# Decay attention, then a GELU MLP: the last 64 queries of batches 3 to 7 as one AV run of two heads side by side

## The chip, the core and the metric

The kernel runs on one core of one Trainium2 chip. The metric is the device time of one execution in microseconds (us). A profile records one execution: when each engine was busy, what ended its idle time, and what the DMA engines moved. The engines are TensorE (in the profile PE, its weight loads PEld), VectorE (DVE), ScalarE (ACT), GpSimd (POOL) and SyncE (SP), which issues most of the DMAs. Each engine works through its own instructions in their order; engines wait for each other through semaphores. Matmuls write to PSUM, which has eight banks of 512 fp32 columns; everything else lies in SBUF.

## The reference

Eight batches, eight heads, 576 tokens, 64 columns a head. Scores get a decay from the cumulative sum of log f and a causal mask; the attention's output, all heads side by side, is the input x of an MLP with exact GELU (512 to 2048 to 512).

```python
log_f = np.log(np.clip(f, 0.0001, 1.0))
cum = np.cumsum(log_f, axis=-1)
decay = cum[:, :, :, None] - cum[:, :, None, :]
scores = np.where(causal, -1e9, scale * q @ k.T + decay)
attn = softmax(scores)                      # over the keys
x = (attn @ v).transpose(0, 2, 1, 3).reshape(B * S, H * D)
out = gelu(x @ w_in) @ w_out
```

The decay of a query cancels in the softmax. The kernel multiplies v by a weight per key instead (`wT`) and carries the weight itself as a 65th column of v, which gives the softmax's sum.

## The kernel before

**Blocks.** 576 tokens are 4.5 blocks of 128. The key blocks and the query blocks begin at `K0 = [0, 128, 256, 384, 448]`: the fifth block of queries, 448 to 575, repeats 64 queries of the fourth. gemm1 of a batch takes the first 512 tokens of x (`TC`). The last 64 tokens (`TL`) of all eight batches are gathered in one tile `tails`, 8 x 64 = 512 columns for each of four groups of 128 rows of x, and go through the MLP at the very end, as a ninth "batch" (`gemm1(B, ...)`, `gemm2(B)`).

**Order.** The schedule is written out by hand: instructions are issued in the order of the program, and each engine keeps its part of it. Batches 0 and 1 have code of their own (`first_attention`, `second_attention`). From batch 2 on, `attention(b)` does, for each of four pairs of heads `i`, four score tiles (`scores`, L319 on TensorE, exp on ScalarE at L329, causal mask on GpSimd at L331). Between them come pieces of gemm2 of the batch before (`take(fill, n)`, L509). From batch 3 on, AV of all four pairs follows: `av(0)`, `av_both(b, 1)`, `av_both(b, 2)`, `av(3)`, then the last eleven steps of gemm2, then gemm1 of this batch (`gemm1_open`, then `gemm1`, all at L405).

**AV.** `attend` (L350) does, for a head and query block m, one matmul for each key block n up to m: the stationary operand is 128 columns of the tile of exponentials `e`, the moving one the 65 columns of weighted v. So the blocks take 1 + 2 + 3 + 4 + 5 = 15 matmuls a head. `normalize` (L363, L364) or the end of `av_both` (L838, L839) divides on VectorE into a tile `x` in SBUF; the pool of these tiles has four. `x_dma` (L389) then has SP issue a transposing DMA of five blocks of 128x128 into `xT`, pair by pair. `x_tail` (L395) is a copy on GpSimd of the last 64 columns of `xT` into `tails`, behind all transposes.

**Who holds PSUM.** `s_psum` has two slots of two banks: score tiles, the outputs of `av_both`, and in `gemm1_open` four accumulators. `o_psum` has two banks (`av`, and `spare()` in gemm1), `m_psum` two (gemm2, gemm1). `gemm1_open` takes two slots of `s_psum`, two of `o_psum` and one of `m_psum` at once for seven column groups, and does the first two of the four row groups of x for six of them, so that the transposes of the later pairs have time to land. A copy of gemm2's last group (`put_off`, L906) is held back behind the divisions of AV, and the last addition and store of gemm2 (L533, L537) come after it.

**Batch 0** already treats its last 64 queries apart (`attend_tail`, L689): two heads of a pair write to the lower and the upper 64 partitions of one bank, with stationary operands of 64 columns. `tail_0` transposes that on TensorE.

Of the kernel before, what the change touches and what calls it, by code (L numbers as in the profile page):

```python
# [9 lines left out]
FP32 = mybir.dt.float32  # L10
BF16 = mybir.dt.bfloat16
Act = mybir.ActivationFunctionType
Alu = mybir.AluOpType
PSUM = bass.MemoryType.PSUM

P = 128
S = 576
D = 64
H = 8
HP = 4  # L20
NBLK = 5
K0 = [0, 128, 256, 384, 448]
TC = 512
# [18 lines left out]
def where(n, m):  # L42

    q = K0[m]
    for t, parts in enumerate(STILES):
        c = 0
        for nn, q0, w in parts:
            if nn == n and q0 <= q and q + P <= q0 + w:
                return t, c + q - q0
            c += w  # L50
    raise KeyError((n, m))
# [3 lines left out]
def kernel(  # L55
# [10 lines left out]
    nc = tc.nc  # L66
    B = q.shape[0]
# [3 lines left out]
    n_dm = d_model // P  # L71
    n_ff = d_ff // P
    n_sub = TC // P
    XC = NBLK * P
    TL = S - TC
# [5 lines left out]
    consts = ctx.enter_context(tc.tile_pool(name="consts", bufs=1))  # L81
# [5 lines left out]
    x_pool = ctx.enter_context(tc.tile_pool(name="x", bufs=4))  # L87
# [3 lines left out]
    s_psum = ctx.enter_context(tc.tile_pool(name="s_psum", bufs=2, space=PSUM))  # L91
# [119 lines left out]
                ps[:, 0:w], warm[:, 0:P], warm[:, 0:w], start=True, stop=True  # L211
            )

    tails = consts.tile([P, n_dm, TC], BF16)


    def transposes_first(b, i, pool, tag, both=(0, 1), parts=1):
# [58 lines left out]
    vw_of = {}  # L276
# [20 lines left out]
    e_of = {}  # L297
# [43 lines left out]
    o_of, x_of, xT_of = {}, {}, {}  # L341

    def attend(b, i, h, ms, pool=o_psum, tag="o"):
        if (b, i, h) not in o_of:
            o_of[b, i, h] = pool.tile([P, NBLK, D + 1], FP32, tag=tag, name="o")
        o = o_of[b, i, h]
        for m in ms:
            for n in range(m + 1):
                t, c = where(n, m)
                nc.tensor.matmul(  # L350
                    o[:, m, :],
                    e_of[b, i, t][:, h, c : c + P],
                    vw_of[b][:, 2 * i + h, n, :],
                    start=(n == 0),
                    stop=(n == m),
                )

    def normalize(b, i, h):
        if (b, i) not in x_of:
            x_of[b, i] = x_pool.tile([P, NBLK, 2, D], BF16, tag="x", name="x")  # L360
        o = o_of[b, i, h]
        r = x_pool.tile([P, NBLK], FP32, tag="r", name="r")
        nc.vector.reciprocal(r, o[:, :, D])  # L363
        nc.vector.tensor_tensor(  # L364
            x_of[b, i][:, :, h, :],
            o[:, :, 0:D],
            r.unsqueeze(2).to_broadcast([P, NBLK, D]),
            Alu.mult,
        )

    def xT(b):
        if b not in xT_of:
            xT_of[b] = xT_pool.tile([P, n_dm, XC], BF16, tag="xT", name="xT")
        return xT_of[b]
# [11 lines left out]
        copy(xT(b)[:, i, :], ps)  # L386

    def x_dma(b, i):
        nc.sync.dma_start_transpose(  # L389
            xT(b)[:, i, :].rearrange("d (m p) -> d m p", p=P),  # L390
            x_of[b, i].rearrange("p m h d -> p (m h d)"),
        )

    def x_tail(b):
        nc.gpsimd.tensor_copy(tails[:, :, b * TL : (b + 1) * TL], xT(b)[:, :, XC - TL :])  # L395


    g_of = {}

    def gemm1(c, ffb, kts=range(4), ps=None, act=True):  # L400
        src = xT(c) if c < B else tails
        if ps is None:
            ps = m_psum.tile([P, TC], FP32, tag="m", name="ps1")
        for kt in kts:
            nc.tensor.matmul(  # L405
                ps,
                w_in_sb[:, kt, ffb * P : (ffb + 1) * P],
                src[:, kt, 0:TC],
                start=(kt == 0),
                stop=(kt == n_dm - 1),  # L410
            )
        if n_dm - 1 in kts and act:
            gelu(c, ffb, ps)
        return ps

    def spare():
        return o_psum.tile([P, TC], FP32, tag="o", name="ps1")

    def gelu(c, ffb, ps):
        if c not in g_of:  # L420
            g_of[c] = [
                g_pool.tile([P, TC], BF16, tag=f"g{n}", name=f"g{n}")
                for n in range(n_ff)
            ]
        nc.scalar.activation(g_of[c][ffb], ps, Act.Gelu)  # L425
# [159 lines left out]
    def gemm2_third():  # L585
        yield from gemm2_second(0)
        yield from gemm2_rows(0, PLAN_0)
        yield from gemm2_rows(1, PLAN_1)

    def take(gen, n):  # L590
        for _ in range(n):
            if next(gen, "end") == "end":
                return
# [68 lines left out]
            x_of[0, i] = x_pool.tile([P, NBLK, 2, D], BF16, tag="x", name="x")  # L662
        divide(x_of[0, i][:, 0 : TC // P, h, :], o, TC // P)

    def divide(x, o, n):
        r = x_pool.tile([P, NBLK], FP32, tag="r", name="r")
        nc.vector.reciprocal(r[:, 0:n], o[:, 0:n, D])
        nc.vector.tensor_tensor(
            x,
            o[:, 0:n, 0:D],  # L670
            r[:, 0:n].unsqueeze(2).to_broadcast([P, n, D]),
            Alu.mult,
        )

    def to_xT_0(i, copy):
        ps = m_psum.tile([P, TC], BF16, tag="m", name="ps_x")
        for m in range(TC // P):
            nc.tensor.transpose(
                ps[:, m * P : (m + 1) * P], x_of[0, i][:, m, :, :], ident_bf
            )  # L680
        copy(xT(0)[:, i, 0:TC], ps)
# [18 lines left out]
    def tail_0():  # L700
        ps = o_psum.tile([P, HP, TL], BF16, tag="o", name="ps_x")
        for i in range(HP):
            for h in range(2):
                d = slice(h * D, (h + 1) * D)
                nc.tensor.transpose(
                    ps[d, i, :], x_of[0, "tail"][d, i, :], ident_bf[d, d]
                )
        nc.vector.tensor_copy(tails[:, :, 0:TL], ps)

    def first_attention():  # L710

# [116 lines left out]
    def av_both(b, i):  # L828


        st = s_psum.tile([P, 2, 512], FP32, tag="s", name="o2")
        both = st[:, :, 0 : NBLK * (D + 1)].rearrange("p h (m d) -> p h m d", m=NBLK)
        for h in range(2):
            o_of[b, i, h] = both[:, h]
            attend(b, i, h, (0, 1, 2, 3, 4))
        x_of[b, i] = x_pool.tile([P, NBLK, 2, D], BF16, tag="x", name="x")
        r = x_pool.tile([P, 2, NBLK], FP32, tag="r2", name="r2")
        nc.vector.reciprocal(r, both[:, :, :, D])  # L838
        nc.vector.tensor_tensor(  # L839
            x_of[b, i].rearrange("p m h d -> p h m d"),  # L840
            both[:, :, :, 0:D],
            r.unsqueeze(3).to_broadcast([P, 2, NBLK, D]),
            Alu.mult,
        )
        x_dma(b, i)
# [21 lines left out]
    def attention(b):  # L867


        fill = gemm2_third() if b == 2 else gemm2_rows(b - 1, PLAN)  # L870
        counts = FILL_2 if b == 2 else FILL

        def av(i, n=0):
            for h in range(2):
                attend(b, i, h, (0, 1, 2, 3, 4))
                normalize(b, i, h)
                if h == 0:
                    take(fill, n)
            x_dma(b, i)

        for i in range(HP):
            for t in range(4):
                scores(b, i, t)
                take(fill, counts[i][t])
                if t == 1 and b == 2 and i > 0:
                    av(i - 1)
                    if i == 1:
                        load_v(3)
                if b == 2 and (i, t) == (0, 3):
                    weigh_v(b, 2)  # L890
                    weigh_v(b, 3)
                if b > 2 and i == 0 and t == 1:
                    load_v(b + 1)
                if b > 2 and t == 0 and i < 2:
                    transpose_dma(b + 1, 4 * i, 4 * i + 4)
                if b == 2 and t == 1 and i == 1:
                    transpose_dma(3, 0, 4)
        if b == 2:
            take(fill, 4)
            av(HP - 1)  # L900
        else:
            av(0)
            av_both(b, 1)
            av_both(b, 2)
            av(3)
            put_off.pop()()  # L906
        if b == 2:
            take(fill, 4)
            transpose_dma(3, 4, 8)
        take(fill, 999)  # L910

        if b == 2:
            pss = [gemm1(b, ffb, (0, 1)) for ffb in range(2)]
            pss += [spare(), spare()]
            for ffb in range(2):
                gemm1(b, ffb, (2,), pss[ffb])
            for ffb in (2, 3):
                gemm1(b, ffb, (0, 1, 2), pss[ffb])
            for ffb in range(4):
                gemm1(b, ffb, (3,), pss[ffb])  # L920
            more = s_psum.tile([P, 2, 512], FP32, tag="s", name="ps1")
            gemm1(b, 4, ps=more[:, 0, :])
        else:
            gemm1_open(b)
        if b + 1 < B:
            untangle(b + 1, 0)
            weigh_v(b + 1, 0)
        x_tail(b)

    def second_attention():  # L930

# [133 lines left out]
```

## Time and profile before

| what | before |
|---|---|
| time, median of 3 runs (lowest to highest) | 332.75 us (332.35 to 337.22) |
| the profiled execution: its time, its span | 332.24 us, 330.5 us |
| granted TensorE clock | 0.999 |
| AV, L350, on TensorE | 840 matmuls, 29.0 us busy |
| batch 0's tail, L689, on TensorE | 40 matmuls, 0.8 us busy |
| gemm1, L405, from x and from the tails | 512 matmuls, 114.0 us; 64 matmuls, 14.3 us |
| GpSimd's copies into the tails, L395 | 7, 3.4 us busy, 29.1 us idle before them |
| transposes of x, L389, on SP | 24, 2.7 us from issue to landing (median) |

The busy time of a group is the time in which at least one of its instructions was running. Matmuls overlap in the pipeline: one of 512 columns lasts 379 ns in the records, while the next starts 216 ns after it. So costs on TensorE are read from start to start. The chain that ended last follows the work back from the end of the execution, at each step to what released it; an engine that is not on it can be late by some amount without any effect.

### The profile page before, as it was taken

What the parts mean: (1) busy time and instruction counts of PE and PEld (TensorE: products, weight loads), DVE (VectorE), ACT (ScalarE), POOL (GpSimd) and SP (SyncE); (2) the same over time, 40 slices, a digit from 0 to 9 for tenths busy, and PEclk for the clock granted to TensorE, in tenths of its full rate; (3) what the DMA queues carried; (4) which work ended last, traced back from release to release, by engine and by line L of the source; (5) the groups of instructions that cost most, each with busy time, mean ns of one, the idle gap of its engine ahead of it and who ended that gap; (6) DMA issues with size and microseconds to landing.
All of it is one profiled execution on the core that took longest, in us unless ns stands there. A gap on an engine that the chain in (4) does not pass through costs nothing.

```text
span 330.5 us, 8129 instructions
## 1 busy us (share of the span) xinstructions
PE 322.2 (97%) x3327; PEld 173.0 (52%) x3327; DVE 184.6 (56%) x412; ACT 203.0 (61%) x296; POOL 134.5 (41%) x260
## 2 busy tenths in 40 slices
PE   8999999999999999999999999999999999999995
PEld 4664555445554467445744565456645574444443
DVE  5952766754649637993599359954995370010011
ACT  4986886965526894289718980899078926305600
POOL 8997873067346153525344443635152500000000
PEclk9999999999999999999999999999999999999999
DMA  7999999959999699399968996699600141020022
GB/s 125 194 195 220 208 193 147 207 122 220 199 194 178 101 227 140 84 157 179 213 94 117 189 219 117 94 172 236 122 15 2 66 96 48 0 97 32 0 54 76
DMA packets 94949, 44.19 MB, mean 134 GB/s; under 512 B 74176, under 2 KB 89792, under 8 KB 94912
## 3 DMA queue, kind: packets, MB, share of 16 engines
q1 hardware_dynamic: 77760, 27.16, 42.5%
q0 software_dynamic: 16752, 15.99, 30.3%
q8 instruction: 26, 0.43, 0.6%
q10 hardware_dynamic: 400, 0.52, 0.4%
q14 instruction: 11, 0.09, 0.1%
HBM read 36.85 MB, written 9.44 MB: 140 GB/s over the span
## 4 chain that ended last, share of the span: by engine, by line
PE 94%; ACT 2%; DMA 1%; DVE 1%; issue 1%; SPq 0%; DVEq 0%
PE ps L405 38%; PE ps L509 27%; PE ps L449 8%; PE o L350 8%; PE s L319 6%; DMA xT<-x 1%; PE s L623 1%; PE ps_w L210 1%; ACT e L628 1%; PE ps_f L226 1%; PE ps L573 1%; PE ps L549 1%; PE o L654 1%; ACT e L329 0%; PE ps_x L383 0%
## 5 line engine op out<-in xcount | busy, mean ns | idle before, releaser
L425 ACT ACTIVATE g<-ps 128x512 bf16<-128x512 f32 x138 | 75.8, 618 | 87.3 <-PE ps L405 86.1
L405 PE MATMUL ps<-xT,w_in_sb 128*128 128x512 bf16 x512 | 114.0, 379 | 0.8 <-DMA xT<-x 0.6
L509 PE MATMUL ps<-w_out_sb,g 64*128 64x512 bf16 (+1 forms) x751 | 106.3, 376 | 0.0
L329 ACT ACTIVATE e<-s 128x896 bf16<-128x896 f32 x112 | 87.8, 836 | 14.4 <-PE s L319 9.9
L405 PEld LDWEIGHTS <-w_in_sb 128*128 128x128 bf16 x576 | 55.3, 98 | 67.2 <-issue 2.1
L331 POOL TENSOR_SCALAR_AFFINE_SELECT e<-e 128x256 bf16<-128x256 bf16 (+1 forms) x135 | 49.1, 383 | 76.6 <-ACT e L329 76.3
L509 PEld LDWEIGHTS <-g 64*128 64x128 bf16 (+1 forms) x751 | 42.6, 94 | 32.2 <-issue 1.3
L288 POOL TENSOR_TENSOR vw<-v_sb,wT 128x640 bf16<-128x640 f32 (+1 forms) x30 | 38.3, 1276 | 29.4 <-DMA v_sb<-in_v_dram 14.9
L269 DVE COPY qT<-tq 64x288 bf16<-64x288 bf16 x96 | 44.1, 459 | 3.5 <-DMA tq<-q 2.0
L523 DVE COPY ot<-ps 128x512 f32<-128x512 f32 x20 | 13.8, 692 | 52.8 <-PE ps L509 52.8
L269 DVE COPY kT<-tk 64x288 bf16<-64x288 bf16 x96 | 38.3, 399 | 2.7 <-DMA tk<-k 1.1
L319 PE MATMUL s<-qT,kT 64*128 64x256 bf16 (+1 forms) x336 | 37.8, 275 | 0.8 <-DVE kT L241 0.6
L458 DVE COPY ot<-ps 128x512 f32<-128x512 f32 (+2 forms) x9 | 5.7, 632 | 49.5 <-PE ps L449 49.5
L350 PEld LDWEIGHTS <-e 128*128 128x128 bf16 x840 | 27.9, 98 | 4.3 <-issue 2.4
L350 PE MATMUL o<-vw,e 128*128 128x65 bf16 x840 | 29.0, 194 | 0.0
L319 PEld LDWEIGHTS <-kT 64*128 64x128 bf16 x336 | 18.1, 94 | 19.8 <-issue 4.0
L449 PE MATMUL ps<-w_out_sb,g 128*128 128x512 bf16 (+2 forms) x144 | 28.0, 355 | 0.0
L449 PEld LDWEIGHTS <-g 128*128 128x128 bf16 x144 | 13.4, 97 | 14.5
L533 DVE TENSOR_TENSOR ot<-ot,ps 128x512 f32<-128x512 f32 x27 | 18.6, 688 | 4.1 <-PE ps L509 1.8
L364 DVE TENSOR_TENSOR x<-o,r 128x320 bf16<-128x320 f32 x36 | 17.7, 492 | 1.2
L395 POOL COPY tails<-xT 128x256 bf16<-128x256 bf16 x7 | 3.4, 486 | 29.1 <-DMA xT<-x 27.2
L405 PE MATMUL ps<-tails,w_in_sb 128*128 128x512 bf16 x64 | 14.3, 378 | 0.0
(92 smaller groups left out, 200.0 us busy)
## 6 DMA issues: line engine op xcount, KB each, us to landing
out_dram<-ot SPq DMA_DIRECT2D x32, 256.0 KB, 2.5
v_sb<-in_v_dram SPq DMA_DIRECT2D x24, 256.0 KB, 4.8
q<-in_q_dram POOLq DMA_DIRECT2D x6, 576.0 KB, 6.3
k<-in_k_dram POOLq DMA_DIRECT2D x6, 576.0 KB, 8.5
v_sb<-in_v_dram POOLq DMA_DIRECT2D x17, 128.0 KB, 6.0
w_in_sb<-in_moe_w_in_dram POOLq DMA_DIRECT2D x4, 512.0 KB, 7.6
w_out_sb<-in_moe_w_out_dram POOLq DMA_DIRECT2D x4, 512.0 KB, 7.9
v_sb<-in_v_dram SPq DMA_DIRECT2D x6, 128.0 KB, 4.8
```

The source lines that it names most:

```text
L269: nc.vector.tensor_copy(rows[:, odd], src[odd * D : (odd + 1) * D, 2 * i + h].rearrange("d j p -> d p j"),)
L288: eng.tensor_tensor(vw(b)[:, hs, n0:n1, 0:D], v_sb[:, hs, n0:n1, :], w.unsqueeze(3).to_broadcast([P, 2, n1 - n0, D]), Alu.mult,)
L319: nc.tensor.matmul(to, *ab, start=half < 0, stop=half == 1 or not masked)
L329: nc.scalar.activation(et[:, :, z:c], st[:, :, z:c], Act.Exp, scale=scale)
L331: nc.gpsimd.affine_select(out=et[:, :, c0 + z : c0 + P], in_=et[:, :, c0 + z : c0 + P], compare_op=Alu.is_ge, fill=0.0, base=z, pattern=[[ ...
L350: nc.tensor.matmul(o[:, m, :], e_of[b, i, t][:, h, c : c + P], vw_of[b][:, 2 * i + h, n, :], start=(n == 0), stop=(n == m),)
L364: nc.vector.tensor_tensor(x_of[b, i][:, :, h, :], o[:, :, 0:D], r.unsqueeze(2).to_broadcast([P, NBLK, D]), Alu.mult,)
L405: nc.tensor.matmul(ps, w_in_sb[:, kt, ffb * P : (ffb + 1) * P], src[:, kt, 0:TC], start=(kt == 0), stop=(kt == n_dm - 1),)
L425: nc.scalar.activation(g_of[c][ffb], ps, Act.Gelu)
L449: nc.tensor.matmul(pss[ts][:, c0:c1], g_of[c][kt][:, ts * P : (ts + 1) * P], w_out_sb[:, kt, c0:c1], start=(kt == 0), stop=(kt == n_ff - 1),)
L509: nc.tensor.matmul(banks[r], g_of[c][kt][rows, ts * P : (ts + 1) * P], w_out_sb[rows, kt, :], start=kt == (steps.index("r") if r else 0), ...
L533: nc.vector.tensor_tensor(ot, ot, bank, Alu.add)
```

## The change

In batches 3 to 7 (`blocks(b)`) AV, the division and the transpose of a pair cover four blocks, 512 queries, without the fifth. A new function `tail(b)` comes after `av(3)` and four more steps of gemm2. It computes the last 64 queries of all eight heads as one run into one bank of a slot of `s_psum`: 64-column stationary operands, head pairs 0 and 1 to the lower 64 partitions, head pairs 2 and 3 to the upper. One division follows, and one transposing DMA of two blocks, straight into `tails`. For that, `tails` is laid out anew: `[P, 2, B, 2, TL]`, that is, for each of two row groups `i` the batches one after another, and for each batch the 64 columns of row group `i` and then those of row group `i + 2`. gemm1 of the tails then reads, for a row group, eight runs of 64 columns that begin 128 columns apart. The copies into `tails` of batches 0 to 2 (on VectorE at L708 for batch 0, on GpSimd at L395 for 1 and 2) write the new layout; for batches 3 to 7 the copy on GpSimd is gone. `divide` is the function that batch 0 already used, moved up.

```diff
-    tails = consts.tile([P, n_dm, TC], BF16)
+    tails = consts.tile([P, 2, B, 2, TL], BF16)
...
     def normalize(b, i, h):
         if (b, i) not in x_of:
             x_of[b, i] = x_pool.tile([P, NBLK, 2, D], BF16, tag="x", name="x")
-        o = o_of[b, i, h]
+        nm = blocks(b)
+        divide(x_of[b, i][:, 0:nm, h, :], o_of[b, i, h], nm)
+
+    def blocks(b):
+        return NBLK - 1 if b > 2 else NBLK
+
+    def divide(x, o, n):
         r = x_pool.tile([P, NBLK], FP32, tag="r", name="r")
-        nc.vector.reciprocal(r, o[:, :, D])
+        nc.vector.reciprocal(r[:, 0:n], o[:, 0:n, D])
...
     def x_dma(b, i):
+        nm = blocks(b)
         nc.sync.dma_start_transpose(
-            xT(b)[:, i, :].rearrange("d (m p) -> d m p", p=P),
-            x_of[b, i].rearrange("p m h d -> p (m h d)"),
+            xT(b)[:, i, 0 : nm * P].rearrange("d (m p) -> d m p", p=P),
+            x_of[b, i][:, 0:nm].rearrange("p m h d -> p (m h d)"),
         )
+    def tail(b):
+        st = s_psum.tile([P, 2, 512], FP32, tag="s", name="o3")
+        o = st[:, 0, 0 : HP * (D + 1)].rearrange("p (k d) -> p k d", k=HP)
+        for i in range(HP // 2):
+            for h in range(2):
+                for n in range(NBLK):
+                    t, c = where(n, NBLK - 1)
+                    for a in range(2):
+                        ii = 2 * a + i
+                        nc.tensor.matmul(
+                            o[a * TL : (a + 1) * TL, 2 * i + h, :],
+                            e_of[b, ii, t][:, h, c + P - TL : c + P],
+                            vw_of[b][:, 2 * ii + h, n, :],
+                            start=(n == 0),
+                            stop=(n == NBLK - 1),
+                        )
+        x = x_pool.tile([P, NBLK, 2, D], BF16, tag="x", name="x")
+        x = x.rearrange("p k h d -> p (k h) d")[:, 0:HP]
+        divide(x, o, HP)
+        nc.sync.dma_start_transpose(
+            tails[:, :, b].rearrange("d i a t -> d i (a t)"),
+            x.rearrange("p k d -> p (k d)"),
+        )
...
-                src[:, kt, 0:TC],
+                xT(c)[:, kt, 0:TC] if c < B else tails[:, kt % 2, :, kt // 2, :],
...
-            attend(b, i, h, (0, 1, 2, 3, 4))
+            attend(b, i, h, range(nm))          # in av_both; in av: range(blocks(b))
...
             av_both(b, 1)
             av_both(b, 2)
             av(3)
+            take(fill, 4)
+            tail(b)
             put_off.pop()()
...
-        x_tail(b)
+        if b == 2:
+            x_tail(b)
```

More of the change, by code (lines that the diff above doesn't have):

```diff
@@ L360, in normalize @@
             x_of[b, i] = x_pool.tile([P, NBLK, 2, D], BF16, tag="x", name="x")
-        o = o_of[b, i, h]
+        nm = blocks(b)
[3 more added lines that the diff above has]
+    def divide(x, o, n):
         r = x_pool.tile([P, NBLK], FP32, tag="r", name="r")
-        nc.vector.reciprocal(r, o[:, :, D])
+        nc.vector.reciprocal(r[:, 0:n], o[:, 0:n, D])
         nc.vector.tensor_tensor(
-            x_of[b, i][:, :, h, :],
-            o[:, :, 0:D],
-            r.unsqueeze(2).to_broadcast([P, NBLK, D]),
+            x,
+            o[:, 0:n, 0:D],
+            r[:, 0:n].unsqueeze(2).to_broadcast([P, n, D]),
             Alu.mult,
@@ L388, in x_dma, with by_half @@
     def x_dma(b, i):
+        nm = blocks(b)
         nc.sync.dma_start_transpose(
-            xT(b)[:, i, :].rearrange("d (m p) -> d m p", p=P),
-            x_of[b, i].rearrange("p m h d -> p (m h d)"),
+            xT(b)[:, i, 0 : nm * P].rearrange("d (m p) -> d m p", p=P),
[23 more added lines that the diff above has]
+            x.rearrange("p k d -> p (k d)"),
         )
     def x_tail(b):
-        nc.gpsimd.tensor_copy(tails[:, :, b * TL : (b + 1) * TL], xT(b)[:, :, XC - TL :])
+        nc.gpsimd.tensor_copy(tails[:, :, b], by_half(xT(b)[:, :, XC - TL :]))
+    def by_half(t):
+        return t.rearrange("d (a i) t -> d i a t", a=2)
     g_of = {}
     def gemm1(c, ffb, kts=range(4), ps=None, act=True):
-        src = xT(c) if c < B else tails
         if ps is None:
@@ L663, in attend_0 @@
         divide(x_of[0, i][:, 0 : TC // P, h, :], o, TC // P)
[L665 to L673, printed above, removed]
     def to_xT_0(i, copy):
@@ L707, in tail_0 @@
                 )
-        nc.vector.tensor_copy(tails[:, :, 0:TL], ps)
+        nc.vector.tensor_copy(tails[:, :, 0], by_half(ps))
     def first_attention():
@@ L831, in av_both @@
         st = s_psum.tile([P, 2, 512], FP32, tag="s", name="o2")
-        both = st[:, :, 0 : NBLK * (D + 1)].rearrange("p h (m d) -> p h m d", m=NBLK)
+        nm = blocks(b)
+        both = st[:, :, 0 : nm * (D + 1)].rearrange("p h (m d) -> p h m d", m=nm)
         for h in range(2):
             o_of[b, i, h] = both[:, h]
-            attend(b, i, h, (0, 1, 2, 3, 4))
+            attend(b, i, h, range(nm))
         x_of[b, i] = x_pool.tile([P, NBLK, 2, D], BF16, tag="x", name="x")
-        r = x_pool.tile([P, 2, NBLK], FP32, tag="r2", name="r2")
+        r = x_pool.tile([P, 2, nm], FP32, tag="r2", name="r2")
         nc.vector.reciprocal(r, both[:, :, :, D])
         nc.vector.tensor_tensor(
-            x_of[b, i].rearrange("p m h d -> p h m d"),
+            x_of[b, i][:, 0:nm].rearrange("p m h d -> p h m d"),
             both[:, :, :, 0:D],
-            r.unsqueeze(3).to_broadcast([P, 2, NBLK, D]),
+            r.unsqueeze(3).to_broadcast([P, 2, nm, D]),
             Alu.mult,
@@ L874, in av @@
             for h in range(2):
-                attend(b, i, h, (0, 1, 2, 3, 4))
+                attend(b, i, h, range(blocks(b)))
                 normalize(b, i, h)
```

## Prediction

> **What bounds the kernel now.** I read the busy shares first, then the chain of work that ended last, then the timeline around the places that the diff touches. TensorE is busy for 97% of the span, and the chain lies on it for 94%:
>
> ```profile
> PE 322.2 (97%) x3327; PEld 173.0 (52%) x3327; DVE 184.6 (56%) x412; ACT 203.0 (61%) x296; POOL 134.5 (41%) x260
> PE 94%; ACT 2%; DMA 1%; DVE 1%; issue 1%; SPq 0%; DVEq 0%
> ```
>
> The same chain in order of time, at the end of batch 3's attention (first three lines), of batch 4's, and in the last gemm1 (columns: start, length in us, what):
>
> ```profile
> 126.15 2.02 PE o L350 x60
> 128.28 4.63 DMA xT<-x
> 133.04 13.97 PE ps L405 x64
> ...
> 161.33 3.91 PE o L350 x120
> 165.24 2.37 PE ps L509 x11
> 167.61 13.81 PE ps L405 x64
> ...
> 298.46 14.14 PE ps L405 x64
> ```
>
> In batches 4 to 7 the AV block (L350), the last eleven steps of gemm2 (L509) and gemm1 (L405) follow each other on TensorE with nothing between. So a microsecond taken from AV is a microsecond off the span, until the next thing that gemm1 needs is late. Batch 3 shows what that is: its gemm1 waits for the first transposed x. The list of waits has 0.6 us of it.
>
> **AV, removed.** The timeline gives groups with their starts. Batch 4:
>
> ```profile
> 161.26 3.98 PE L350 MATMUL o<-vw,e 128*128 128x65 bf16 x120
> 163.36 6.28 SPq L389 DMA_TRANSPOSE xT<-x  x4
> 165.07 2.54 PE L509 MATMUL ps<-w_out_sb,g 128*128 128x512 bf16 x11
> 167.45 4.91 PE L405 MATMUL ps<-xT,w_in_sb 128*128 128x512 bf16 x22
> ```
>
> 120 AV matmuls take 165.07 - 161.26 = 3.81 us from start to start, 31.75 ns each. The fifth block costs 5 of the 15 matmuls of each of 8 heads: 40 x 31.75 ns = **1.27 us** go.
>
> **AV, added.** The tail has 40 matmuls, with 64-column stationary operands that go alternately to the lower and the upper 64 output partitions. Batch 0 runs exactly this form (L689), between gemm1 matmuls:
>
> ```profile
> 22.33 3.21 PE L405 MATMUL ps<-xT,w_in_sb 128*128 128x512 bf16 x14
> 25.47 0.72 PEld L689 LDWEIGHTS <-e 128*64 128x64 bf16 x40 [0.42 <-issue]
> 25.47 0.83 PE L689 MATMUL o<-vw,e 128*64 128x65 bf16 x40
> 26.24 1.04 PE L405 MATMUL ps<-xT,w_in_sb 128*128 128x512 bf16 x4
> ```
>
> 512-column matmuls start every 13.81 / 64 = 0.216 us. The last of the 14 starts at 22.33 + 3.21 - 0.38 (mean duration) = 25.16, so without the block the next would start at 25.38; it starts at 26.24. The block costs **0.86 us**, both changes of form included (without those about 0.65 us, 16 ns each). Its neighbours in batches 3 to 7 are 128*128 matmuls too, so I take 0.86.
>
> The sum on TensorE: -1.27 + 0.86 = -0.41 us a batch, **-2.05 us** in five batches.
>
> A rule speaks against it. The Trainium skill, TensorEngine Tiling (Array Packing), Restrictions and Gotchas, says that column tiling excludes the fast weight load; TensorE: Matmul & The Clock Gate, LDWEIGHTS, puts a load at columns / 1.2 ns. By these, 40 loads of 64 columns in a row would take an estimated 2.1 us a batch, and the kernel would end near 337. The L689 row disagrees: 40 loads are over in 0.72 us.
>
> **VectorE, and the slots it frees.** I count from the start of AV (161.26 in batch 4) and put the new durations on it. VectorE divides in order. The rows for 128x5 and 128x320 (186 and 492 ns) become those of batch 0, 128x4 and 128x256 (179 and 424 ns); a pair took 0.64 us (161.94 to 162.58) and takes about 0.58. Two heads at once (216 + 824 ns, 1.00 us a pair) lose 128 columns, about 0.13 us. First head: matmuls end at 0.32, division starts 0.2 later as before (0.52), second 1.1, both heads of pair 1 end at 2.6, of pair 2 at 3.5, pair 3 at 4.7, the tail's division at 5.2. TensorE: AV to 2.54, four steps of gemm2 to 3.40, tail to 4.27, seven steps to 5.78, then gemm1 (before: 6.19).
>
> - The tail's bank is the one of av_both's first pair: free at 2.6, wanted at 3.40.
> - gemm1's second pair of banks is the tail's: free at 5.2, wanted at 5.78 + 0.43 = 6.21.
> - The put-off copy (L906, 0.68 us) and the last sum (L533, 0.69) come behind the tail's division, end about 7 and are wanted by the seventh bank at 5.78 + 12 x 0.216 = 8.4.
>
> All hidden: cost nothing, with 0.8, 1.0 and 1.4 us of cover. What goes beyond it is paid five times.
>
> **A new wait.** The ring of x tiles has four; a batch now takes five. The tail's x takes the tile of pair 0, so its division waits until pair 0's transpose has landed, and behind it on VectorE stand the put-off copy, the last sum and the next batch's copies of q and k (wanted some 13 us later). The transposes of pair 0 start 2.1 us after AV does (163.36); by the DMA view they took 4.6, 2.5, 3.8, 3.9 and 3.9 us to land in batches 3 to 7. In the new order they start at about 1.8 and land at 4.2 to 6.4. At 3.9 us: 5.7, the division ends at 6.2, just as the bank is wanted. And gemm1's first matmul needs the same transpose at 5.78. Batch 7 shows how tight that is now:
>
> ```profile
> 266.57 5.96 SPq L389 DMA_TRANSPOSE xT<-x  x4
> 270.58 5.37 PEld L405 LDWEIGHTS <-w_in_sb 128*128 128x128 bf16 x26 [0.24 <-DVE ot L906]
> ```
>
> The transpose lands at 266.57 + 3.9 = 270.5, and the weight load starts at 270.58 (the releaser that is named, L906, is done as well by then). The transposes shrink from five blocks to four: those of q, 12 blocks, land in 4.2 us (median) and those of x, 5 blocks, in 2.7, so a block is worth some 0.2 us. Start 0.3 earlier plus 0.2 sooner stands against gemm1's 0.41: the balance keeps. I take 0; the ends are -0.6 (batch 3's wait gone) and +1.35 in all (second rival).
>
> **SP.** Issuing one transpose occupies SP for 1.2 us (1201 to 2351 ns), four or five blocks alike. The fifth stands behind pair 3's, ahead of the last store (169.73, 0.53 us), which is 0.9 us later and which nobody awaits. Pair 3's x is issued about 5.7, lands by 9.3 (3.6 us, batch 4) and is wanted at 5.78 + 21 x 0.216 = 10.3. Nothing.
>
> **GpSimd.** Its copy into the tails (L395, 0.49 us) goes in five batches, and with it waiting on transposes (27.2 us over six). What stands behind, weighing v and the loads of q and k, runs some 4 us earlier: the load issued at 174.50 comes near 170.3, when pair 3's transpose is about landed. Nobody on the path waits for either. Zero; if a load did delay that transpose, there is 1 us of cover.
>
> **The last gemm1.** Its moving operand is now eight runs of 64 columns, 128 apart, in place of one run of 512; 64 matmuls. No matmul of the trace reads runs. Upper end: each break costs what a matmul has besides its columns. 65 columns take 31.75 ns and 512 take 216, so a column is 0.41 ns and the rest 5 ns; 7 x 5 x 64 = 2.25 us. Lower end 0, as a pattern of equal size can't gain. The nearest rows are ScalarE's reads of two runs, 704 ns for 2x320 and 1024 for 2x512, which lie on a line without a step of its own (0.83 ns an element). I take 0.
>
> **Sum.** 332.24 us (profiled execution, span 330.5) - 2.05 = 330.2 us. The median of the runs, 332.75, stands 0.5 above that execution and their lowest, 332.35, 0.1 above it; I give 330.3.
>
> **Rivals.**
> 1. *The gain also takes the wait of batch 3, or the changes of form cost less in these places:* up to 0.6 + 5 x 0.21 more. 329.2. For it: the transposes start earlier. Chance 0.08.
> 2. *The first transpose becomes the end.* If it lands when it does now, counted from AV's start (6.8, 4.6, 5.9, 6.0, 6.0 us, by what else is on the DMA engines), gemm1 can start at 7.0 in batch 3 (no gain), 5.78 in batch 4, and about 6.1 in the others (0.1 gained each): 0.41 + 0.3 = 0.7 us gained, **331.5**. Against: it is issued earlier and is smaller. Chance 0.17.
> 3. *Slower: the runs of the last gemm1.* At the upper end 332.2 - 2.05 + 2.25, **332.5**, 0.2 over the profiled execution. It decides from 32 ns a matmul, 4.6 ns a break. Against: no engine's rows show such a step. Chance 0.08.
> 4. *The change doesn't do what it says:* the two column halves don't run side by side, each matmul takes 31.75 ns, and the changes of form are extra: 5 x 0.21 = 1.05, **333.3**. Against: L689. Chance 0.03.
> 5. *The 64-column loads are not hidden.* One after another at their own mean of 111 ns they would take 4.4 us a batch: 5 x (4.4 - 1.27) = +15.9, **348**. Against: again L689. Chance 0.02. This is what the rule of the Trainium skill's TensorEngine Tiling (Array Packing) would come to here; the skill's own figure gives the 337 above.
>
> The forecast has the remaining 0.62, by itself 329.8 to 330.9. The range, **329.0 to 332.6**, takes in rivals 1 to 3. Faster or slower by over 2% (6.6 us, about what a measurement of this kernel can tell from no change) has 0.01 and 0.02; within 2% 0.97.
>
> **What would show it.** L350 falls from 840 to 640 matmuls, and a new 128*64 group of 200 takes under 0.9 us a batch between gemm2 steps; start of AV to start of gemm1 falls from 6.19 to about 5.8 us in batches 4 to 7; the chain keeps that order without a DMA piece (rival 2 has one in several batches); the last gemm1 stays near 14.1 us (rival 3: 16.4). I would be wrong through a wait that I placed under cover: a VectorE delay at the tail's bank or at gemm1's third bank.

## The result and the profile after

| what | before | after |
|---|---|---|
| time, median of 15 runs each (lowest to highest) | 332.83 us (331.88 to 337.22) | 330.44 us (329.47 to 334.16) |
| ratio | | 0.9928, 95% interval 0.9904 to 0.9952 |
| the profiled execution: its time, its span | 332.24, 330.5 us | 330.52, 328.8 us |
| AV, L350 | 840 matmuls, 29.0 us busy | 640 matmuls, 22.6 us busy |

The change makes the kernel 2.4 us faster (0.9928 x 332.83 = 330.4; by the interval 1.6 to 3.2 us). The forecast was 330.3 us, 2.05 us less. Now and then a run falls into a slower state (337.22 in the table); the ratios, here and below, leave such runs out, so they need not be the quotient of the medians.

The page of the changed kernel, busy shares and the chain by engine:

```profile
PE 318.2 (97%) x3295; PEld 169.9 (52%) x3327; DVE 180.5 (55%) x422; ACT 203.3 (62%) x296; POOL 131.5 (40%) x255
PE 86%; DMA 8%; POOL 3%; issue 1%; ACT 0%; DVE 0%; another core or an unknown queue 0%; POOLq 0%
```

TensorE is busy for the same share of the span as before. The 8% of DMA in the chain are loads of k, q and v in the first 40 us, which this execution waited for. Batch 1, the same code in both kernels but for the layout of its copy into the tails, took 34.05 us in the profile of before and 34.91 in this one; over the eleven profiles whose batch 1 has this code it ranges from 33.9 to 35.2 us.

The chain in order of time (start, length, what), batch 3, batch 4, and the last gemm1:

```profile
127.47 2.62 PE o L350 x80
130.15 0.81 PE ps L544 x3
130.96 0.77 PE o L412 x40
131.74 1.40 PE ps L544 x6
133.38 10.76 PE ps L440 x49
...
161.68 2.62 PE o L350 x80
164.36 0.81 PE ps L544 x3
165.17 0.77 PE o L412 x40
165.94 1.40 PE ps L544 x6
167.40 10.74 PE ps L440 x49
...
297.20 14.14 PE ps L440 x64
```

Line numbers have moved: gemm2 was L509 and is L544, gemm1 was L405 and is L440, the tail is L412. (Of four steps of gemm2 ahead of the tail three are recorded, of seven behind it six.) The AV block is down to 80 matmuls, the tail's 40 stand between the steps of gemm2, and gemm1 follows at once in batch 4, and 0.23 us later in batch 3. The last gemm1, with its eight runs, takes 14.14 us to the digit of before.

From the start of AV (first L350) to the start of gemm1, us, read from the timelines of all profiles, with those of the experiments below:

| kernel | batch 3 | 4 | 5 | 6 | 7 |
|---|---|---|---|---|---|
| before | 6.96 | 6.19 | 6.19 | 6.19 | 6.19 |
| before, once more | 6.24 | 6.19 | 6.19 | 6.19 | 6.19 |
| after | 5.97 | 5.78 | 5.78 | 5.78 | 5.78 |
| after, once more | 6.19 | 5.78 | 5.78 | 6.01 | 5.78 |
| five x tiles | 6.26 | 5.78 | 5.78 | 5.78 | 5.78 |
| halves in turn | 6.32 | 6.32 | 6.32 | 6.32 | 6.32 |
| tail at once | 6.29 | 5.78 | 5.77 | 5.77 | 5.77 |
| tail late | 5.81 | 5.78 | 6.30 | 5.83 | 5.78 |
| batch 2 as well | 6.46 | 5.78 | 5.78 | 5.78 | 5.78 |
| batches 1 and 2 as well | 6.40 | 5.78 | 5.78 | 5.78 | 5.78 |
| the same with a brake | 6.98 | 5.78 | 5.78 | 6.16 | 5.78 |
| 128 instructions more | 6.67 | 5.80 | 6.37 | 5.78 | 5.78 |
| 256 instructions more | 6.24 | 5.78 | 5.78 | 5.78 | 5.78 |

From the first score matmul of batch 3 to the last matmul the two profiles of before take 214.52 and 213.80 us, those of after 211.93 and 212.39: 2.0 us less on average, without the chance of the loads at the start. How late batch 3 is differs from profile to profile and is in these numbers.

Inside batch 4 of the changed kernel (timeline; start, length, engine, what):

```profile
161.61 2.69 PE L350 MATMUL o<-vw,e 128*128 128x65 bf16 x80
163.39 6.20 SPq L396 DMA_TRANSPOSE xT<-x  x4
165.10 0.84 PE L412 MATMUL o<-vw,e 128*64 128x65 bf16 x40
166.23 0.42 DVE L370 TENSOR_TENSOR x<-o,r 128x256 bf16<-128x256 f32 x1
166.57 0.68 DVE L934 COPY ot<-ps 128x512 f32<-128x512 f32 x1
167.40 1.89 PE L440 MATMUL ps<-xT,w_in_sb 128*128 128x512 bf16 x8
```

Counted from 161.61: the first transpose is issued at 1.78 (forecast 1.8), the tail starts at 3.49 (3.40 and the change of form), its division ends at 5.04 (5.2), gemm1 starts at 5.79 (5.78).

### The profile page after: what moved, and what is told of

Its sections match the earlier page's. It is cut to its first block, busy times and chain, and to the rows that moved or that the text cites. A ratio compares the mean times of both kernels' runs of the same rounds, so it can differ in the third digit from the quotient of the medians.

```text
span 328.8 us, 8087 instructions
## 1 busy us (share of the span) xinstructions
PE 318.2 (97%) x3295; PEld 169.9 (52%) x3327; DVE 180.5 (55%) x422; ACT 203.3 (62%) x296; POOL 131.5 (40%) x255
## 4 chain that ended last, share of the span: by engine, by line
PE 86%; DMA 8%; POOL 3%; issue 1%; ACT 0%; DVE 0%; another core or an unknown queue 0%; POOLq 0%
PE ps L440 35%; PE ps L544 27%; PE ps L484 8%; PE o L350 6%; PE s L319 6%; DMA q<-in_k_dram 3%; DMA k<-in_k_dram 3%; DMA v_sb<-in_v_dram 2%; PE o L412 1%; PE ps L608 1%; POOL q L120 1%; PE ps L584 1%; POOL k L120 1%; POOL w_in_sb L184 1%; POOL vw L288 1%
## 5 line engine op out<-in xcount | busy, mean ns | idle before, releaser
L440 PE MATMUL ps<-xT,w_in_sb 128*128 128x512 bf16 x499 | 113.0, 379 | 1.5 <-DVE xT L706 0.3
L544 PE MATMUL ps<-w_out_sb,g 64*128 64x512 bf16 (+1 forms) x737 | 104.4, 376 | 0.8 <-issue 0.5
L440 PEld LDWEIGHTS <-w_in_sb 128*128 128x128 bf16 x576 | 55.2, 98 | 66.7 <-issue 2.6
L544 PEld LDWEIGHTS <-g 64*128 64x128 bf16 (+1 forms) x751 | 42.1, 94 | 31.3 <-issue 1.3
L269 DVE COPY kT<-tk 64x288 bf16<-64x288 bf16 x96 | 35.2, 367 | 5.3 <-DMA tk<-k 3.6
L370 DVE TENSOR_TENSOR x<-o,r 128x256 bf16<-128x256 f32 (+1 forms) x50 | 22.3, 446 | 4.3 <-DMA xT<-x 2.7
L350 PEld LDWEIGHTS <-e 128*128 128x128 bf16 x640 | 21.5, 98 | 4.3 <-issue 2.4
L350 PE MATMUL o<-vw,e 128*128 128x65 bf16 x640 | 22.6, 194 | 0.0
L440 PE MATMUL ps<-tails,w_in_sb 128*128 128x512 bf16 x64 | 14.3, 378 | 0.0
L369 DVE RECIPROCAL r<-o 128x4 f32<-128x4 f32 (+1 forms) x50 | 8.9, 179 | 8.1 <-PE o L350 3.9
```

The source lines that it names most:

```text
L269: nc.vector.tensor_copy(rows[:, odd], src[odd * D : (odd + 1) * D, 2 * i + h].rearrange("d j p -> d p j"),)
L350: nc.tensor.matmul(o[:, m, :], e_of[b, i, t][:, h, c : c + P], vw_of[b][:, 2 * i + h, n, :], start=(n == 0), stop=(n == m),)
L370: nc.vector.tensor_tensor(x, o[:, 0:n, 0:D], r[:, 0:n].unsqueeze(2).to_broadcast([P, n, D]), Alu.mult,)
L440: nc.tensor.matmul(ps, w_in_sb[:, kt, ffb * P : (ffb + 1) * P], xT(c)[:, kt, 0:TC] if c < B else tails[:, kt % 2, :, kt // 2, :], start=(k ...
L544: nc.tensor.matmul(banks[r], g_of[c][kt][rows, ts * P : (ts + 1) * P], w_out_sb[rows, kt, :], start=kt == (steps.index("r") if r else 0), ...
```

## The experiments

Each is the changed kernel with one edit, unless said otherwise. Times are compared with before in the same call: 332.85 us (31 runs) for the first four, 332.87 (23) for five x tiles, batch 2, batches 1 and 2 and the kernel before once more, 332.93 (14) for the brake and the two shifts.

**The halves of the tail in turn.** This asks what makes a matmul of the tail cost 16 ns.

```diff
-        for i in range(HP // 2):
-            for h in range(2):
-                for n in range(NBLK):
-                    t, c = where(n, NBLK - 1)
-                    for a in range(2):
+        for a in range(2):
+            for i in range(HP // 2):
+                for h in range(2):
+                    for n in range(NBLK):
```

> The changed kernel with the tail's loops turned round: first the 20 matmuls of the lower 64 columns of the array, then the 20 of the upper, instead of lower and upper in turn; same matmuls, same operands. Theory: in turn, the loads and matmuls of one half run beside those of the other, which is what makes one cost 16 ns. Within one half they follow each other like the 128-column ones, at 31.75 ns: the block of 40 takes 40 x 31.75 + 0.21 = 1.48 us instead of 0.86, start of AV to start of gemm1 6.4 us instead of 5.78, in all +3.1 us on the changed kernel's 330.4. Rival A: a matmul with half the columns is cheap by itself, whatever its neighbour; nothing changes (0.86 us). Rival B: within one half a 64-column load isn't hidden at all and takes what the Trainium skill (TensorE: Matmul & The Clock Gate, LDWEIGHTS) estimates, 53 ns: the block takes some 2.3 us, +7 us in all.

Measured 332.17 us, 0.9975 (0.9946 to 1.0003) of before: most of the gain is gone. Timeline of its batch 4, TensorE:

```profile
163.07 1.02 PE L544 MATMUL ps<-w_out_sb,g 128*128 128x512 bf16 x4
164.03 1.38 PE L412 MATMUL o<-vw,e 128*64 128x65 bf16 x40
165.34 1.68 PE L544 MATMUL ps<-w_out_sb,g 128*128 128x512 bf16 x7
```

The 40 starts lie (1.38 - 0.194) / 39 = 30.4 ns apart, against (0.84 - 0.194) / 39 = 16.6 ns in the changed kernel (0.194 us is the duration of one). AV to gemm1 takes 6.32 us in every batch, 0.54 more. So the gain comes from the two halves working beside each other; within one half a 64-column matmul costs about what a 128-column one does (31.75). In turn, neighbours also write to different outputs, which could be the reason instead. The single records speak against it: in the changed kernel the starts come in pairs, a lower and an upper matmul 0 to 10 ns apart; with one half at a time 28 to 36 ns lie between starts after the first, also where the output changes (32 to 35 ns), and short steps come only where lower half gives way to upper. Rival A falls, and so does B: 53 ns a load is not to be seen even within one half.

**The tail at once.** The cover of the tail's bank.

```diff
-            take(fill, 4)
             tail(b)
```

> The changed kernel without the four gemm2 steps between the last AV and the tail; they run after the tail. Theory: the tail's bank is free when the first two-head division ends, 2.56 us after AV's start (measured), and the tail now wants it at 2.54, plus some 0.1 us from the end of a division to a start on TensorE: 0.1 to 0.2 us of idle time in each of five batches, +0.5 to +1.0 us in all; start of AV to start of gemm1 5.9 to 6.0 us. Rival: the division is no limit and the four steps cover nothing, 0; or the tail's earlier division helps gemm1 where it is late (batch 3), -0.2.

330.66 us, 0.9944 (0.9921 to 0.9968). The theory's loss didn't come. Batch 4, AV from 162.01:

```profile
163.88 0.69 DVE L865 TENSOR_TENSOR x<-o,r 128x512 bf16<-128x512 f32 x1
164.64 0.84 PE L412 MATMUL o<-vw,e 128*64 128x65 bf16 x40
```

The bank is free at 164.57 and the tail starts 0.07 us later, at 2.63. It was wanted at 2.54; but a tail after gemm2 also starts 0.09 us after its turn (3.49 for 3.40), for the change of form. The wait lies within that pause. The four steps cover nothing here, by a hair.

**The tail late.** Ten steps ahead of it, one behind.

```diff
-            take(fill, 4)
+            take(fill, 10)
             tail(b)
```

> The changed kernel with ten gemm2 steps ahead of the tail instead of four, one after it. Theory: the tail's matmuls end at 2.54 + 2.16 + 0.86 = 5.56 us after AV's start, its division at about 6.4, and gemm1's third accumulator, which takes the tail's bank, is wanted at 6.21: some 0.2 us lost in each batch, shown as idle time of TensorE after gemm1's second matmul, +1 us in all. Rival: other work covers it and nothing changes; or the last sum of gemm2, which now stands behind a later division, becomes the wait (at the seventh accumulator, wanted at 8.4), over 0.5 us a batch.

331.39 us, 0.9943 (0.9912 to 0.9974). In its batch 4:

```profile
165.57 0.84 PE L412 MATMUL o<-vw,e 128*64 128x65 bf16 x40
166.67 0.42 DVE L370 TENSOR_TENSOR x<-o,r 128x256 bf16<-128x256 f32 x1
167.15 1.41 PEld L440 LDWEIGHTS <-w_in_sb 128*128 128x128 bf16 x8 [0.48 <-DVE x L370]
```

The weight load for gemm1's third accumulator waits for the tail's division, as expected. From the start of gemm1 to the next batch's scores it takes 14.03 and 14.07 us in batches 3 and 4, against 13.93 and 13.91 in the changed kernel: 0.10 and 0.16 us lost, about two thirds of what was expected. Whole runs don't resolve so little. The 6.30 us of its batch 5 have another cause, which is taken up with the landing times below.

**The changed kernel once more.**

> The changed kernel once more, for a second profile. Theory: start of AV to start of gemm1 is 5.78 us in batches 4 to 7 and the last gemm1 takes as long as before, in every execution. In batch 3 it depends on where an instruction fetch falls: when one falls into the first transpose of x, that lands after about 4 us instead of 2.4, and gemm1 starts at about 6.0 or later; when none does, at 5.78. Rival: batch 3 is late in every execution by the same 0.2 us, because of its loads of v and of q and k.

330.26 us, 0.9926 (0.9886 to 0.9965). Batches 4, 5 and 7 are at 5.78 again; batch 6 is not, at 6.01, so "in every execution" was too much. Batch 3 was late in both, and here its first transpose stands in the chain, just ahead of gemm1:

```profile
128.81 4.17 DMA xT<-x
```

**Five x tiles**, against the new wait of VectorE.

```diff
-    x_pool = ctx.enter_context(tc.tile_pool(name="x", bufs=4))
+    x_pool = ctx.enter_context(tc.tile_pool(name="x", bufs=5))
```

> The changed kernel with five x tiles in the ring instead of four, so that the tail's division no longer waits for the first transpose. Theory: the wait (1.35 us of VectorE in batch 3) costs TensorE only where that transpose is late, a few tenths in batch 3 at gemm1's third accumulator; start of AV to start of gemm1 stays 5.78 us in batches 4 to 7, in all 0 to -0.3 us. Rival: the wait delays something in every batch (the put-off copy, the copies of q and k of the next batch), -0.3 us a batch, -1.5 us in all.

330.15 us, 0.9888 (0.9828 to 0.9949, a wide interval). The table says more: 5.78 in batches 4 to 7, as without it, and batch 3 at 6.26, within what it shows from run to run. The rival's 1.5 us are not there. In the changed kernel the wait was real in batch 3:

```profile
133.34 0.42 DVE L370 TENSOR_TENSOR x<-o,r 128x256 bf16<-128x256 f32 x1 [1.35 <-DMA xT<-x]
133.38 0.83 PE L440 MATMUL ps<-xT,w_in_sb 128*128 128x512 bf16 x3 [0.24 <-remote]
```

VectorE waited 1.35 us for the first transpose, and gemm1, which waits for the same one, started 0.04 us after the division did.

**Batch 2 as well.** Can the same be had in batch 2?

```diff
-        return NBLK - 1 if b > 2 else NBLK
+        return NBLK - 1 if b > 1 else NBLK
...
             take(fill, 4)
             av(HP - 1)
+            tail(b)
...
-        if b == 2:
-            x_tail(b)
```

> The changed kernel with batch 2 treated like batches 3 to 7: four blocks, the tail right behind the last AV, no copy into the tails on GpSimd. Theory: the same sum as in the other batches, -1.27 + 0.86 = -0.41 us, as long as the transposes of x land in time; 330.0. Rival: in batch 2 only the last pair's transpose is close to gemm1, and nothing covers the tail's bank: the tail waits or gemm1 does, and the gain is gone, 0.

332.39 us, 0.997 (0.9943 to 0.9997): slower than the changed kernel. Batch 2 takes 45.85 us, against 45.45 in both kernels. In batch 2, AV of three pairs stands between score tiles and steps of gemm2, and there the ten matmuls less save 0.06 us, not 0.32, a pair (5.24 for 5.30). Timeline of one such place:

```profile
84.80 0.69 DVE L568 TENSOR_TENSOR ot<-ot,ps 128x512 f32<-128x512 f32 x1
85.27 1.30 PE L544 MATMUL ps<-w_out_sb,g 64*128 64x512 bf16 x8
85.55 0.52 PEld L544 LDWEIGHTS <-g 64*128 64x128 bf16 x6 [0.37 <-issue]
```

gemm2 seems to need the bank that VectorE's addition frees at 85.49. AV was the cover for that; the shorter AV ends before it, and TensorE's next six weight loads come from 85.55 on (the profile names no releaser). The tail's 0.86 us are paid in full. The rival had the outcome. Neither had the reason, which this trace suggests and no run of its own confirms.

**Batches 1 and 2 as well.** Also `blocks` from batch 1 on, four blocks in the transposes on TensorE, and:

```diff
         gemm1_begin(1, both)
-        x_tail(1)
+        tail(1)
```

> Batches 1 and 2 treated like batches 3 to 7. In batch 1 x is transposed on TensorE, so four of 20 transposes at about 55 ns go too; its tail comes after the first gemm1 groups. Theory: -0.41 (batch 2) - 0.41 - 0.22 (batch 1) = -1.0 us on the changed kernel, 329.4. Rival: VectorE or the slots of PSUM are the limit in batch 1, and the tail there adds a wait: 0 to +1 us.

334.02 us, 1.0008 (0.997 to 1.0046): the whole gain is gone. Its chain, GpSimd's timeline and TensorE's, around batch 2's gemm1:

```profile
99.80 6.28 DMA xT<-x
```
```profile
99.86 0.82 POOL L120 DMA_DIRECT2D q<-in_q_dram  x1
```
```profile
106.12 11.47 PE L441 MATMUL ps<-xT,w_in_sb 128*128 128x512 bf16 x52 [3.32 <-DMA xT<-x]
```

The last pair's transpose went out at 99.80, and at 99.86 GpSimd issued the loads of q and k. In the changed kernel's second profile they are issued at 102.88: GpSimd waits until 99.45 for the copy into the tails of batch 2, and the copy waits for all transposes.

**The same with a brake.**

```diff
             weigh_v(b + 1, 0)
+        if b == 2:
+            g = x_pool.tile([P, 1], BF16, tag="gate", name="gate")
+            nc.gpsimd.tensor_copy(g, xT(b)[:, HP - 1, 0:1])
```

> The kernel in which batches 1 and 2 are treated like 3 to 7, with one thing more: after GpSimd's first weighing for batch 3 it copies one column of the last pair's transposed x of batch 2, and so waits for that transpose, as its copy into the tails did. Theory: without the copy into the tails GpSimd issued the loads of q and k (1.2 MB) at 99.9 us, as the last pair's transpose went out at 99.8, and that transpose took 6.3 us and held gemm1 for 3.3 us. With the wait back, the loads come some 3 us later, the transpose lands in 2.3 to 2.6 us, and the 3.3 us of idle time in batch 2's gemm1 are gone: about 330.5 to 331. Rival: the transpose is late because SP issued it late and an instruction fetch or the stores delayed it; the idle time stays.

331.94 us, 0.9963 (0.9935 to 0.9992), where 330.5 to 331 had been expected. The last transpose lands in 2.35 us instead of 6.28, and batch 2 takes 46.37 us instead of 50.86. So the loads, now issued at 104.70, had held it, and GpSimd's copy had kept them apart. From batch 2's gemm1 to the next scores it is still 14.51 us, against 13.99 in the changed kernel; the reason stays open. Batch 2 doesn't gain (46.37 us for 45.45). Batch 1's 34.5 us without the brake and 34.9 with it lie within the 33.9 to 35.2 that the unchanged one shows, so no gain is to be seen there. The changed kernel stays the best one.

**Where batch 3's wait comes from: the kernel before once more, and two shifts.** In the profile of before the first transpose of batch 3 took 4.6 us to land. The DMA view shows 16 KB transfers of instructions on a queue of their own; 26 in both kernels, which makes one for every 256 of TensorE's 3327 matmuls and 3327 weight loads. The shifts add warm-up matmuls at the start:

```diff
         warm_up(9)
+        warm_up(64, D)          # or 128
```

> The kernel before once more, for a second profile. Theory: start of AV to start of gemm1 is 6.19 us in batches 4 to 7 in every execution; in batch 3 it is 6.96 or 6.19, with or without an instruction fetch that falls into its first transpose. Rival: batch 3 is at 6.96 in every execution, so that its wait is the kernel's own.

> The changed kernel with 64 more warm-up matmuls (64 columns, 128 TensorE instructions with their loads) at the very start, nothing else. Theory: the 16 KB instruction transfers are TensorE's own instructions, 256 at a time (26 of them for 6647 instructions), and the first transpose of a batch lands late when one of them falls into it. With 128 instructions more, each transfer comes 128 instructions earlier in the program. In the changed kernel they fall on the first transpose in batches 3 and 6 (4.0 and 3.7 us to land) and not in 4 and 7 (2.6 and 2.3). Now batches 3 and 6 land within 2.6 us, and gemm1 starts 5.78 us after AV in batch 3, while in batch 4, and perhaps 5 or 7, the first transpose lands after 3 us or more. Rival: batch 3 is late because of its own loads of v, q and k: its first transpose still takes about 4 us, and batch 4's stays at 2.6. The extra warm-up may cost up to 2 us at the start.

> The changed kernel with 128 more warm-up matmuls at the very start, 256 TensorE instructions, one whole instruction transfer. Theory: the transfers fall where they did in the changed kernel: the first transpose is late in batches 3 and 6 (3.5 us and more) and lands within 3.1 us in batches 4, 5 and 7. Rival: a shift in time, not in instructions, moves the pattern, so that this one differs from the changed kernel's as well. The extra warm-up may cost up to 4 us at the start.

The three were run once each: 331.88 us for the kernel before, 333.87 and 334.52 for the shifts with their longer warm-up. Only their profiles are used. With 256 instructions more there are 27 transfers instead of 26.

Landing of the first transpose, us from its issue, and in brackets when an instruction transfer began, us from the same issue, if any did from 0 to 3 us:

| kernel | batch 3 | 4 | 5 | 6 | 7 |
|---|---|---|---|---|---|
| before | 4.63 (1.2) | 2.49 | 3.79 (0.7) | 3.89 (1.3) | 3.90 (1.8) |
| before, once more | 3.91 (1.8) | 2.37 | 3.82 (0.8) | 3.16 (0.5) | 3.90 (1.8) |
| after | 3.96 (1.7) | 2.57 | 3.05 (0.6) | 3.69 (0.8) | 2.34 |
| 128 instructions more | 4.66 (0.6) | 3.89 (0.8) | 4.45 (2.4) | 2.37 | 2.57 (0.0) |
| 256 instructions more | 4.23 (1.8) | 2.30 | 2.59 (0.2) | 3.85 (0.9) | 2.34 |

With a whole transfer's worth of instructions the pattern is that of the changed kernel, batch by batch; with half of it, 4 turns late and 6 on time. One forecast failed: batch 3 stayed late with half a period. Another transfer now met its transpose, 0.6 us after the issue, but there other data also took 64.7% of the DMA engines' time in the 1.2 us from the issue, and which of the two held it isn't settled. In the profile of before, whose batch 3 took 4.63 us, it is: from 128.3 to 129.5 the instruction transfer has 7.1% and everything else 1.2%, so batch 3's own loads aren't needed to explain it. The DMA view of batch 6, from the first transpose's issue for 1.2 to 1.3 us, in the changed kernel (first) and with 128 instructions more:

```profile
q8 instruction: 1, 0.02, 6.6%
...
xT<-x SPq DMA_TRANSPOSE x1, 3.7
```
```profile
xT<-x SPq DMA_TRANSPOSE x1, 2.4
```

The q8 line is the instruction transfer; in the second view there is none. Over all 13 profiles, 65 first transposes: the 34 with a transfer that began 0.5 to 2.4 us after the issue took 3.05 to 4.66 us; of the other 31, 30 took 2.29 to 2.99 and one 3.93. (The limits 0.5 and 2.4 are read off these same profiles.) The one is batch 5 of the late tail: its transpose was issued at 2.23 instead of 1.78, behind two stores, and from 197.18 to 199.5 other data and the transpose took 60.5% of the DMA engines' time. So other traffic, too, seems to delay a transpose.

The kernel before, run again (331.88 us), had its batch 3 at 6.24 instead of 6.96. So its long wait was one execution's, and most of it is not the change's to take: in the two profiles of before batch 3's gemm1 came 0.77 and 0.05 us after it could have, in the two of after 0.19 and 0.41.

## Why the prediction was right

- **AV removed, 1.27 us, and added, 0.86.** Both right: 6.19 became 5.78 us in batches 4 to 7, the forecast to the hundredth. Batch 0's group was the price of the tail because it had the same form and neighbours of the same shape; the halves in turn show that the alternation, too, had to be the same.
- **The sum, 2.05 us.** Measured 2.4 (1.6 to 3.2), and 2.0 by the part from batch 3 on, two profiles each. That the median came within 0.2 us of the forecast 330.3 is in part luck: batch 1 alone varies by over 1 us between executions.
- **VectorE and the slots.** The order of ends held: 5.04 us for the tail's division (5.2), the put-off copy and the sum at 167.60 + 0.69 - 161.61 = 6.7 (7). The cover of the tail's bank, 0.8 us, is there, and not needed: the step was right and its price, had the cover gone, was zero. The 1.0 us of cover at the third accumulator is real, as the late tail shows.
- **The new wait.** "The balance keeps" held in batches 4 to 7 of the first profile. Its terms were off: a block less is worth 0.1 us (the fastest transposes of later pairs landed in 2.40 and land in 2.30), not 0.2. With 0.32 for the earlier start that is 0.42 against the 0.41 of gemm1: the balance keeps with nothing to spare, and batch 6 of the second profile, at 6.01, missed it. I took the landing times for a property of each batch; they depend on where the instruction transfers fall.
- **The rivals.** The first, batch 3's wait gone, came in part in the one pair of profiles (0.99 us gained there instead of 0.41) and hardly in the other (6.24 to 6.19). The second, the transpose as the end, holds in batch 3 of both profiles of the changed kernel and in batch 6 of one; its 331.5 did not come. The third falls: 14.14 us for the last gemm1 in both kernels. The fourth and fifth fall with 16.6 ns a matmul. The rule behind the fifth, in the Trainium skill's TensorEngine Tiling (Array Packing), Restrictions and Gotchas, that column tiling excludes the fast weight load, is not to be seen in these times, nor in the 30.4 ns within one half.
- **GpSimd.** The loads were forecast to come near 170.3 and came at 170.37, 3.06 us after batch 4's last pair was issued and 0.40 ahead of its landing (3.46 us, before 3.61). That this was harmless had 1 us to spare by my count; batch 2 shows what it costs where it hasn't.
- **What would show it:** "without a DMA piece" in the chain was right around AV in the first profile, where the pieces belong to the loads at the start. In the second one batch 3 has such a piece, 4.17 us, so it was not right of every execution.

## What to carry to other kernels

Price a new group of matmuls by a group of the same form, in the same alternation and between the same neighbours, from start to start; here that gave the gain of a batch to a hundredth of a microsecond. Matmuls shortened where TensorE has no slack pay in full. Where they only fill the time until something else is done (in batch 2, it seems, VectorE's addition), shortening them pays little: the same edit was worth 0.41 us in one batch and cost 0.4 in another. Before a copy is deleted, look at what its wait holds back on its engine's queue.

## What I had not expected of the hardware

- Instructions come in 16 KB transfers, by their number one for every 256 of TensorE's, and the DMA view counts them in the time of the same 16 engines that move the data. Where one began 0.5 to 2.4 us after a transpose's issue, it landed late (3.05 to 4.66 us after the issue, against some 2.3). Adding 128 instructions at the start moved which batch was hit, and 256 brought the pattern back.
- Two column halves in alternation cost 16.6 ns a matmul of 65 columns, one half alone 30.4, the full width 31.75.
- A moving operand in eight runs of 64 columns, 128 apart, is read as fast as one of 512.
- Issuing a transposing DMA occupies SP for 1.2 us, whether it has two, four or five blocks of 128x128 (1.20 us for the tail's, 1.19 to 1.23 for four, 1.20 to 1.23 for five in batches 3 to 7, where nothing holds it up).
